# Sparse attention then top-1 MoE on one core: three groups of two score tiles a pair instead of four groups

## The chip, the cores and the metric

The kernel runs on one core of a Trainium2 chip. The metric is device time in microseconds from the first to the last instruction of a launch. Before the change it is 352.2 us, the median of three runs (350.9 to 353.01). The profile is one execution of its own, with a span of 355.5 us and a mean granted TensorE clock of 0.988.

A core has five engines, each with its own in-order queue: PE (matmul; its weight loads are shown as PEld), DVE (vector), ACT (scalar and activation), POOL (GpSimd) and SP (here it issues DMAs). They wait for each other through semaphores.

## The reference

The inputs are q, k and v of 4 batches x 8 heads x 768 positions x 64, and a mixture of 8 experts. Attention looks only at a few chunks of 32 keys. For each query an upper bound of its score with each chunk is made from the chunk's element-wise minimum and maximum, and the six causal chunks of the highest bound are kept:

```python
ub = np.sum(np.maximum(q[:, :, :, None, :] * k_min[:, :, None, :, :], q[:, :, :, None, :] * k_max[:, :, None, :, :]), axis=-1)
...
top_chunks = np.argsort(ub, axis=-1)[..., -top_k:]
...
mask = sel & (pos[:, None] >= pos[None, :])
...
attn = attn / (np.sum(attn, axis=-1, keepdims=True) + 1e-09)
return np.matmul(attn, v).astype(np.float32)
```

The heads are then put side by side into rows of 512. Each of the 3072 rows goes to the one expert with the highest gate logit, a relu MLP 512 to 1024 to 512, and is scaled by that expert's softmax probability.

## The kernel before

**Tiling.** Two heads of one batch make a pair, so there are NP = 16 pairs; i is the pair, hp = i % 4 its place in the batch, n = i + 1 and m = i + 2. A pair's 768 queries are two halves of 384 (qb 0 and 1). The scores are made transposed, keys on the partitions, in seven units u (line 286): units 0 and 1 belong to query half 0, units 2 to 6 to half 1. For each unit:

- `scores(i, u)` (L298, PE) multiplies KTE by QSB into a PSUM tile `ps`, of which there are two. Rows 64 and up of KTE and QSB carry the chunk mask, so a chunk that was not chosen is pushed down inside the same matmul.
- `exps(i, u)` (L314, ACT) takes the exponential into SBUF. Units 0 and 2 go to a tile `Pa` (four buffers), which also becomes the accumulator of the half's denominators; the others go to `Pr`, also four buffers. On blocks of the diagonal POOL then clears what is not causal (L318).
- `av(i, u)` (L331, PE) multiplies by V into `po`, of which there is one PSUM bank, used by half 0 and then by half 1.
- `add(i, u)` (L339, DVE) adds the unit into the accumulator. A `Pr` buffer is free when its `av` and its `add` are done.
- `o_ev(i, qb)` (L346 on DVE, L344 on ACT) copies `po` to an `ot` tile.

**Preparation of later pairs** is mixed in. `k_mm`, `k_v`, `k_a` and `q_mm`, `q_v`, `q_a` transpose k and q of pair m on PE, take chunk maxima and minima on DVE (L197, L198), and copy on DVE, ACT and POOL. Where DVE and ACT both read one PSUM bank, the one that stands second in the code waits for the first. `kse` builds the matrix for the bounds. `ub` (L238, PE) makes the bounds, `ub_a` (L245, ACT) copies them to `ubT`, `sel_mm` (L250, PE) transposes them, `sel_v` (L256, L264, L267, DVE) takes the sixth largest and compares. `mask` (L274, PE) transposes the choice, and `mask_a` (L280, ACT) writes it into the mask rows of QSB, which must be done before that pair's scores 0.

**Routing of earlier pairs** is mixed in too. `ud` (PE) and `ud_a` (L380, ACT) gather the denominators and logits of pair i - 1, `lgp_mm` (L385, PE) transposes them, `lgp_v` (L391, L395, DVE) takes reciprocals and scales the logits, and their sums go to POOL later (`sums_`, L403 and L406). `x_mm` and `x_v` (L415, PE; L420, DVE) write the normalised output rows, half 0 one pair late and half 1 two pairs late. In the pairs with hp = 1 and b > 0, the router pairs 5, 9 and 13, the rows of the batch before get their experts: `logits`, `rank_mm`, `expo` (ACT), `rank_v`, `gates`. Rows are scattered to DRAM by POOL. All transposes and bounds share three PSUM buffers of tag `m`, in the order in which they are asked for.

**Order.** All five engines run under a manual schedule (L807): each executes its instructions in the order in which the Python code records them, so the order of calls in the loop over i is the order of every queue. Before the change, that loop has an inner loop over four groups g: scores 2 and 3; scores 4 and 5, then 6; the mask and AV 4 and 5; and scores 0 and 1 of the next pair with the rest of its preparation and AV 6. The output of one pair is finished while the next one is started.

**After attention**, from about 232 us, gathered rows of each expert go through `up` and `down` (L641, L653). The diff does not touch this part, nor `first_pair`.

Of the kernel before, what the change touches and what calls it, by code (L numbers as in the profile page):

```python
# [24 lines left out]
def kernel(  # L25
# [24 lines left out]
    NP = B * H // 2  # L50
# [108 lines left out]
    late, sums_ = [], []  # L159
# [518 lines left out]
    def pieces(i, n):  # L678
        for _ in range(min(n, npiece[i])):
            load_w(next(wnext))  # L680
            npiece[i] -= 1
# [121 lines left out]
    def run(d, j, name, *a):  # L803
        if j in d:
            d[j][name](*a)

    with tc.manual_schedule(engines={PE, POOL, SP, DVE, ACT}):  # L807
        first_pair()
        early_table = table(True)
        for i in range(NP):  # L810
            b, hp = divmod(i, HP)
            n, m = i + 1, i + 2
            router = hp == 1 and b > 0
            if router:
                logits, expo, gates, rank_mm, rank_v, _ = route[b - 1]
            if i == NP - 1:
                for j in range(2):
                    gather(j)
                    x_in(j)
            for g in range(4):  # L820
                if (i, g) == (0, 0):
                    pass
                elif g == 0:
                    if i < NP - 1 and not (hp == 2 and b > 0):
                        pieces(i, 2 if router else 1)
                    if router:
                        logits()
                    for u in (2, 3):
                        scores(i, u)
                        exps(i, u)  # L830
                    run(rout, i - 2, "x_mm", 1)

                    xv_first = i < NP - 1 and (hp != 2 or b == 0)
                    if xv_first:
                        run(rout, i - 2, "x_v", 1)
                    if i < NP - 1:
                        add(i - 1, 5)
                    add(i - 1, 6)
                    if not xv_first:
                        run(rout, i - 2, "x_v", 1)  # L840
                    av(i, 0)
                    av(i, 1)
                    dve_ot = not router and i < NP - 2
                    if dve_ot or i == NP - 1:
                        o_ev(i, 0, not dve_ot)
                    add(i, 1)
                    run(prep, n, "ub")
                    run(prep, n, "ub_a")
                    if not dve_ot and i < NP - 1:
                        o_ev(i, 0, True)  # L850
                    if i < NP - 1:
                        load(n, "v")
                elif g == 1:
                    for u in (4, 5):
                        scores(i, u)
                        exps(i, u)
                    run(prep, n, "sel_mm")
                    if i > 0:
                        run(prep, m, "k_mm", 0)
                        run(prep, m, "k_a", 0)  # L860
                    if router:
                        rank_mm()
                    run(prep, n, "sel_v")
                    if router:
                        expo()
                        rank_v()
                        gates()
                    if i > 0:
                        run(prep, m, "k_v", 0)
                    av(i, 2)  # L870
                    av(i, 3)
                    add(i, 3)
                    flush(late)
                    if i < NP - 1:
                        pieces(i, 4)
                    scores(i, 6, True)
                    exps(i, 6)
                    if i == NP - 1:
                        for j in (2, 3):
                            gather(j)  # L880
                            x_in(j)
                        pieces(i, 4)
                    run(rout, i - 1, "ud")
                    run(rout, i - 1, "ud_a")
                    if i == NP - 2:
                        next(early_table)
                elif g == 2:
                    if i == 0:
                        run(prep, m, "k_mm", 0)
                    run(prep, n, "mask")  # L890
                    run(prep, n, "mask_a")
                    if i == 0:
                        run(prep, m, "k_v", 0)
                        run(prep, m, "k_a", 0)
                    av(i, 4)
                    av(i, 5)
                    if not router:
                        add(i, 4)
                    if i == NP - 2:
                        for _ in early_table:  # L900
                            pass
                    flush(sums_)
                    if i == NP - 1:
                        meta(0)
                        meta(1)
                        gather(4)
                        gather(5)
                else:
                    run(rout, i - 1, "lgp_mm")
                    run(rout, i - 1, "x_mm", 0)  # L910
                    if n < NP:
                        for u in (0, 1):
                            scores(n, u)
                            exps(n, u)
                    if i == NP - 2:
                        add(i, 5)
                    run(rout, i - 1, "lgp_v")
                    run(rout, i - 1, "x_v", 0)
                    run(prep, m, "k_mm", 1)
                    run(prep, m, "k_v", 1)  # L920
                    run(prep, m, "k_a", 1)
                    for hf in range(2):
                        run(prep, m, "q_mm", hf)
                        run(prep, m, "q_v", hf)
                        run(prep, m, "q_a", hf)
                    if i + 3 < NP:
                        load(i + 3, "k", "q")
                    av(i, 6)
                    o_ev(i, 1, i >= NP - 2)
                    run(prep, m, "kse")  # L930
                    if router:
                        add(i, 4)
                    if hp == 0 and b > 0:
                        flush(sums_)
                if 1 <= hp <= 2 and b > 0 and spread[4 * (hp - 1) + g]:
                    route[b - 1][5](spread[4 * (hp - 1) + g])
        rt = rout[NP - 1]
        r = route[B - 1]

        def nxt(j):  # L940
            meta(j - XB)
            gather(j)

        rout[NP - 2]["x_mm"](1)
        rout[NP - 2]["x_v"](1)
        nxt(6)
        nxt(7)
        flush()
        up(0)
        up(1)  # L950
        rt["ud"]()
        rt["ud_a"]()
        x_in(4)
        up(2)
        x_in(5)
        rt["lgp_mm"]()
        rt["lgp_v"]()
        for hf in range(2):
            rt["x_mm"](hf)
            rt["x_v"](hf)  # L960
        flush()
        nxt(8)
        r[0]()
        r[1]()
        r[2]()
        down(0)
        up(3)
        x_in(6)
        nxt(9)
        r[3]()  # L970
        r[4]()
        meta(6)
        meta(7)
        for _ in table(False):
            pass
        gathers = {3: (10,), 4: (11,), 5: (12, 13)}
        for j in range(1, NS):
            if j == NS - 4:
                up(NS - 1)
            down(j)  # L980
            if j < 3:
                r[5](range(3 * j - 3, 3 * j))
            for k_ in gathers.get(j, (j + 8,) if 5 < j < NS - 8 else ()):
                if k_ > 11:
                    meta(k_ - XB)
                gather(k_)
            if j + 8 >= NS and j + 4 < NS:
                meta(j + 4)
            if j + 3 < NS - 1:
                up(j + 3)  # L990
            if j + 6 < NS:
                x_in(j + 6)

        _, more = nc.values_load_multi_w_load_instructions(  # L994
            late_i[0:1, 0:1], min_val=0, max_val=NB,
            skip_runtime_bounds_check_because="a count of tiles that the table itself adds up")
        with tc.If(more[0] > NS - NA) as _:
            for j in range(NS, JT):
                gather(j)
                x_in(j)  # L1000
                meta(j)
            for j in range(NS, JT):
                up(j)
            for j in range(NS, JT):
                down(j)
# [37 lines left out]
```

The softmax here doesn't subtract the row's maximum and nothing guards it: scores larger than these inputs give would overflow.

## Time and profile before

| | before |
|---|---|
| median of three runs | 352.2 us (350.9 to 353.01) |
| span of the profiled execution | 355.5 us |
| attention loop | to about 232 us |
| from one L391 to the next, ordinary pair | 13.2 to 13.5 us |
| the same, router pairs and those after them | 14.3 to 14.8 us |
| exponential of a unit (L314, ACT) | 0.81 us |
| DVE add of a whole unit (L339) | 0.98 us |
| mask copy (L280, ACT) | 0.69 us, two a pair |

A row of the timeline gives the start, the time covered, engine and line, the operation with what it writes and reads, the number of merged instructions, and in brackets the idle time before it with what ended it. The time of several merged rows is that of their union. [...] A busy PE is not PE at its peak, since the ends of its pipelined matmuls are modelled.

### The profile page before, as it was taken

What the parts mean: (1) busy time and instruction counts of PE and PEld (TensorE: products, weight loads), DVE (VectorE), ACT (ScalarE), POOL (GpSimd) and SP (SyncE); (2) the same over time, 40 slices, a digit from 0 to 9 for tenths busy, and PEclk for the clock granted to TensorE, in tenths of its full rate; (3) what the DMA queues carried; (4) which work ended last, traced back from release to release, by engine and by line L of the source; (5) the groups of instructions that cost most, each with busy time, mean ns of one, the idle gap of its engine ahead of it and who ended that gap; (6) DMA issues with size and microseconds to landing.
All of it is one profiled execution on the core that took longest, in us unless ns stands there. A gap on an engine that the chain in (4) does not pass through costs nothing. (4 is left out here: it accounts for less than half of the span.)

```text
span 355.5 us, 7585 instructions
## 1 busy us (share of the span) xinstructions
PE 329.2 (93%) x2382; PEld 177.2 (50%) x2392; DVE 229.5 (65%) x776; ACT 230.4 (65%) x373; POOL 186.7 (53%) x300
## 2 busy tenths in 40 slices
PE   7889999999999999999999999977995899999992
PEld 7545656556555555555565555534441344444440
DVE  6688999999999999999999999941730000000000
ACT  2588788788796887886887977613323454544551
POOL 8515434536475437284355477583574556655323
PEclk9999999999999999999999999989998999999999
DMA  9998998899585897765979954969694999998962
GB/s 175 205 209 152 167 184 169 153 190 167 104 211 113 161 178 155 152 171 114 186 137 181 182 122 113 209 124 197 137 227 121 227 185 216 194 231 160 216 154 80
DMA packets 132071, 59.83 MB, mean 168 GB/s; under 512 B 122811, under 2 KB 122813, under 8 KB 132032
## 3 DMA queue, kind: packets, MB, share of 16 engines
q1 hardware_dynamic: 120640, 29.91, 43.5%
q0 software_dynamic: 11392, 29.42, 40.0%
q8 instruction: 21, 0.34, 0.4%
q14 instruction: 18, 0.15, 0.1%
HBM read 56.14 MB, written 10.51 MB: 188 GB/s over the span
## 5 line engine op out<-in xcount | busy, mean ns | idle before, releaser
L339 DVE TENSOR_TENSOR Pa<-Pa,Pr 128x768 f32<-128x768 f32 (+2 forms) x109 | 80.5, 742 | 4.3
L318 POOL TENSOR_SCALAR_AFFINE_SELECT Pr<-Pr 128x256 f32<-128x256 f32 x78 | 36.9, 492 | 77.9 <-ACT Pr L314 77.9
L314 ACT ACTIVATE Pr<-ps 128x768 f32<-128x768 f32 x79 | 62.6, 819 | 10.7 <-ACT KTE L203 4.3
L653 PE MATMUL py<-w_all,hT 128*128 x220 | 52.4, 379 | 3.0 <-issue 1.7
L298 PE MATMUL ps<-QSB,KTE 128*128 128x384 bf16 (+4 forms) x352 | 50.4, 283 | 1.5 <-ACT Pr L314 0.2
L661 POOL DMA_INDIRECT out_dram<-y,ti_all x28 | 28.0, 1001 | 37.2 <-ACT y L660 32.1
L298 PEld LDWEIGHTS <-KTE 128*128 128x128 bf16 (+1 forms) x352 | 26.5, 102 | 28.4 <-issue 22.0
L641 PE MATMUL ph<-w_all,KTE 128*128 x116 | 31.1, 413 | 6.3 <-ACT h__3986 L644 3.6
L653 PEld LDWEIGHTS <-hT 128*128 128x128 bf16 x224 | 21.8, 98 | 29.5 <-issue 1.8
L314 ACT ACTIVATE Pa<-ps 128x768 f32<-128x768 f32 x32 | 26.0, 812 | 14.0 <-PE ps L298 12.6
L660 ACT ACTIVATE y<-py,gt_all 128x512 f32<-128x512 f32 x27 | 18.6, 687 | 25.0 <-PE py L653 19.4
L203 ACT ACTIVATE KTE<-pk 64x384 bf16<-64x384 f32 x60 | 29.3, 488 | 7.1 <-DVE kmn L198 6.7
L493 POOL DMA_INDIRECT xs_dram<-xrow,sli x24 | 25.6, 1065 | 7.8 <-issue 5.7
L641 PE MATMUL ph<-w_all,QSB 128*128 x94 | 22.6, 379 | 1.6 <-DMA QSB<-xgqT 1.5
L641 PEld LDWEIGHTS <-KTE 128*128 128x128 bf16 x120 | 12.3, 104 | 23.0 <-issue 9.6
L280 ACT ACTIVATE QSB<-pm 24x640 bf16<-24x640 bf16 x30 | 20.8, 692 | 2.8 <-PE pm L274 2.1
L614 DVE TENSOR_TENSOR ti_all<-xgqA,inv_i 128x1 int32<-128x1 int32 x9 | 1.4, 160 | 30.7 <-DMA xgqA<-xs_dram,grow 26.1
L157 POOL DMA_DIRECT2D w_all<-in_moe_w_dram x32 | 21.1, 663 | 0.0
L197 DVE TENSOR_REDUCE kmx<-pk 128x12 f32<-128x384 f32 x32 | 17.6, 549 | 3.2 <-PE pk L192 3.0
L593 POOL DMA_INDIRECT xgqT<-xs_dram,grow x14 | 14.8, 1058 | 9.1 <-issue 6.2
L593 POOL DMA_INDIRECT xgqA<-xs_dram,grow x14 | 14.4, 1029 | 8.6 <-issue 4.7
L614 DVE TENSOR_TENSOR ti_all<-xgqT,inv_i 128x1 int32<-128x1 int32 x8 | 1.3, 159 | 25.7 <-DMA xgqT<-xs_dram,grow 20.9
(318 smaller groups left out, 635.9 us busy)
## 6 DMA issues: line engine op xcount, KB each, us to landing
w_all<-in_moe_w_dram POOLq DMA_DIRECT2D x32, 512.0 KB
out_dram<-y,ti_all POOLq DMA_INDIRECT x28
t__115<-in_k_dram SPq DMA_DIRECT2D x2, 192.0 KB
t__118<-in_q_dram SPq DMA_DIRECT2D x2, 192.0 KB
t__121<-in_v_dram SPq DMA_DIRECT2D x2, 192.0 KB
t__218<-in_k_dram SPq DMA_DIRECT2D x2, 192.0 KB
t__240<-in_q_dram SPq DMA_DIRECT2D x2, 192.0 KB
t__243<-in_v_dram SPq DMA_DIRECT2D x2, 192.0 KB
```

The source lines that it names most:

```text
L157: nc.gpsimd.dma_start(out=dst, in_=src.rearrange("(c p) f -> p c f" if n < 2 else "(p c) f -> p c f", p=128))
L203: nc.scalar.activation(kte[0:64, hd, ts(hf, 384)], pt[64 * hd:64 * hd + 64, :], AF.Copy, bias=0.0, scale=0.125)
L280: nc.scalar.activation(qsb[64:64 + NCH, hd, 128:S], s["pm"][32 * hd:32 * hd + NCH, 128:S], AF.Copy)
L298: nc.tensor.matmul(ps[ds(h * n, n), hd, ds(c0, w)], lhsT=kte[:, hd, ds(kb * 128 + h * n, n)], rhs=qsb[:, hd, ds(qb * 384 + 384 - w, w)], s ...
L314: nc.scalar.activation(P[:], ps[:, :, 0:384], AF.Exp)
L318: nc.gpsimd.affine_select(out=pd, in_=pd, pattern=[[0, 2], [1, 128]], compare_op=ALU.is_ge, fill=0.0, base=0, channel_multiplier=-1)
L339: nc.vector.tensor_tensor(acc[:, :, 384 - w:384], acc[:, :, 384 - w:384], P[:, :, ds(c0, w)], ALU.add)
L493: d = nc.gpsimd.indirect_dma_start(out=xs_dram[:], out_offset=bass.IndirectOffsetOnAxis(ap=sli[:, u:u + 1], axis=0), in_=bst[b][f"xrow{u % ...
L593: d = nc.gpsimd.indirect_dma_start(out=xg_bufs[j % XB].bitcast(I32), out_offset=None, in_=xs_dram[:], in_offset=bass.IndirectOffsetOnAxis( ...
L641: nc.tensor.matmul(ph[:, fh, :], lhsT=xT[:, c, :], rhs=w_all[:, ds(wo + (c * F + fh * 512), 512)], start=(c == 0), stop=(c == NDC - 1), sk ...
L653: nc.tensor.matmul(py[:], lhsT=hT[:, c, :], rhs=w_all[:, ds(wo + (W1W + c * DM), DM)], start=(c == 0), stop=(c == NFC - 1))
L661: d = nc.gpsimd.indirect_dma_start(out=out[:], out_offset=bass.IndirectOffsetOnAxis(ap=fs[j]["ti"], axis=0), in_=y[:], in_offset=None, bou ...
```

## The change

The four groups of a pair are replaced by three that are written out, with two score tiles and then the AV products of earlier units each. It has four purposes: to put the next scores in front of an AV product, so that PE has work while exponentials and selects of that product are under way; to give the bounds a longer lead, by making those of pair m at the end of pair i where before those of pair n were made in the first group; to put the selection ahead of the adds of unit 6 and 1; and to put the mask's transposes and copies next to scores 4 and 5. The diff, cut to its core (`rows_out` holds the scatters, whose place among the groups stays):

```diff
-for g in range(4):
...
-    elif g == 0:
...
-        for u in (2, 3):
-            scores(i, u)
-            exps(i, u)
-        run(rout, i - 2, "x_mm", 1)
...
-            run(rout, i - 2, "x_v", 1)
-        if i < NP - 1:
-            add(i - 1, 5)
-        add(i - 1, 6)
...
-        av(i, 0)
-        av(i, 1)
...
-            o_ev(i, 0, not dve_ot)
-        add(i, 1)
-        run(prep, n, "ub")
-        run(prep, n, "ub_a")
...
-    elif g == 1:
-        for u in (4, 5):
-            scores(i, u)
-            exps(i, u)
-        run(prep, n, "sel_mm")
-        if i > 0:
-            run(prep, m, "k_mm", 0)
-            run(prep, m, "k_a", 0)
-        if router:
-            rank_mm()
-        run(prep, n, "sel_v")
-        if router:
-            expo()
-            rank_v()
-            gates()
-        if i > 0:
-            run(prep, m, "k_v", 0)
-        av(i, 2)
-        av(i, 3)
-        add(i, 3)
-        flush(late)
...
-        scores(i, 6, True)
-        exps(i, 6)
...
-        run(rout, i - 1, "ud")
-        run(rout, i - 1, "ud_a")
...
-    elif g == 2:
...
-        run(prep, n, "mask")
-        run(prep, n, "mask_a")
...
-        av(i, 4)
-        av(i, 5)
-        if not router:
-            add(i, 4)
...
-        flush(sums_)
...
-    else:
-        run(rout, i - 1, "lgp_mm")
-        run(rout, i - 1, "x_mm", 0)
-        if n < NP:
-            for u in (0, 1):
-                scores(n, u)
-                exps(n, u)
...
-        run(rout, i - 1, "lgp_v")
-        run(rout, i - 1, "x_v", 0)
-        run(prep, m, "k_mm", 1)
-        run(prep, m, "k_v", 1)
-        run(prep, m, "k_a", 1)
-        for hf in range(2):
-            run(prep, m, "q_mm", hf)
-            run(prep, m, "q_v", hf)
-            run(prep, m, "q_a", hf)
...
-        av(i, 6)
-        o_ev(i, 1, i >= NP - 2)
-        run(prep, m, "kse")
-        if router:
-            add(i, 4)
-        if hp == 0 and b > 0:
-            flush(sums_)
+if i > 0:
...
+    for u in (2, 3):
+        scores(i, u)
+        exps(i, u)
+    run(rout, i - 2, "x_mm", 1)
+    run(prep, n, "sel_mm")
+    if i < NP - 1:
+        add(i - 1, 5)
+
+    xv_first = i < NP - 1 and (hp != 2 or b == 0)
+    if xv_first:
+        run(rout, i - 2, "x_v", 1)
+    run(prep, n, "sel_v")
+    if not xv_first:
+        run(rout, i - 2, "x_v", 1)
+    av(i, 0)
+    av(i, 1)
+    o_ev(i, 0, not dve_ot)
+    add(i - 1, 6)
+    add(i, 1)
...
+for u in (4, 5):
+    scores(i, u)
+    exps(i, u)
+if i == 0:
+    run(prep, n, "sel_mm")
+    run(prep, n, "sel_v")
+else:
+    run(prep, m, "k_mm", 0)
+    run(prep, m, "k_a", 0)
+    run(prep, n, "mask")
+    run(prep, n, "mask_a")
+    if router:
+        rank_mm()
+        expo()
+        rank_v()
+        gates()
+    run(prep, m, "k_v", 0)
+av(i, 2)
+av(i, 3)
+add(i, 3)
+flush(late)
...
+scores(i, 6, True)
+exps(i, 6)
...
+run(rout, i - 1, "ud")
+run(rout, i - 1, "ud_a")
...
+run(rout, i - 1, "lgp_mm")
+run(rout, i - 1, "x_mm", 0)
+if not router:
+    add(i, 4)
...
+flush(sums_)
...
+run(rout, i - 1, "lgp_v")
+run(rout, i - 1, "x_v", 0)
+run(prep, m, "k_mm", 1)
+if n < NP:
+    scores(n, 0)
+    exps(n, 0)
+    scores(n, 1)
+run(prep, m, "k_v", 1)
+run(prep, m, "k_a", 1)
+for hf in range(2):
+    run(prep, m, "q_mm", hf)
+    run(prep, m, "q_v", hf)
+    run(prep, m, "q_a", hf, 0)
+if n < NP:
+    exps(n, 1)
+for hf in range(2):
+    run(prep, m, "q_a", hf, 1)
...
+run(prep, m, "kse")
+av(i, 4)
+av(i, 5)
+av(i, 6)
+o_ev(i, 1, i >= NP - 2)
+run(prep, m, "ub")
+run(prep, m, "ub_a")
+if router:
+    add(i, 4)
+if hp == 0 and b > 0:
+    flush(sums_)
```

The order of calls that follows from it, for an ordinary pair: scores 2 and 3; x of pair i - 2; transposes and selection for n; AV 0 and 1 and their copy; adds of unit 6 of pair i - 1 and of unit 1; scores 4 and 5; the first k half of m; the mask of n; AV 2 and 3; scores 6; `ud` and `lgp` of pair i - 1; the second k half; scores 0 and 1 of n; q of m with the exponential of unit 1 between its copies; AV 4, 5 and 6; bounds of m.

## Prediction

> **What bounds the kernel now.** I read the page for the engines' shares, then the stages, then the timeline of one ordinary pair (pair 3), each step beside the code.
>
> ```profile
> PE 329.2 (93%) x2382; PEld 177.2 (50%) x2392; DVE 229.5 (65%) x776; ACT 230.4 (65%) x373; POOL 186.7 (53%) x300
> ```
>
> Over the span only PE looks full. By stage it is different (columns: stage, its length, busy PE, PEld, DVE, ACT, POOL, then clock, DMA share, GB/s):
>
> ```profile
> 60.00:80.00 20.00, 19.86 (x174) 10.97 (x170) 18.80 (x60) 17.07 (x30) 8.40 (x16) 1.00 0.89 174
> 300.00:320.00 20.00, 19.89 (x93) 9.07 (x93) 1.37 (x13) 9.55 (x13) 11.85 (x12) 1.00 0.96 206
> ```
>
> In the attention stage, which is all that the diff edits, DVE is busy 18.8 of 20 us. From 33 to 232 us it idles 11.4 us, of which 8.4 us are 570 gaps of 15 ns on average between neighbours, and only 2.9 us are gaps with an outside releaser. PE's 19.9 says less: its records overlap (four matmuls of 0.54 and 0.49 us fit in 0.87 us). So DVE sets the pace of a pair, 13.5 us, and PE and ACT run ahead of it. Timeline of one pair:
>
> ```profile
> 62.80 1.53 ACT L314 ACTIVATE Pr<-ps 128x768 f32<-128x768 f32 x2
> 63.92 0.45 DVE L256 TENSOR_TENSOR ubm<-pt,cbias 128x288 f32<-128x288 f32 x1
> ...
> 65.72 0.81 ACT L314 ACTIVATE Pr<-ps 128x768 f32<-128x768 f32 x1 [0.54 <-ACT KTE L203]
> ...
> 66.61 1.48 POOL L318 TENSOR_SCALAR_AFFINE_SELECT Pr<-Pr 128x256 f32<-128x256 f32 x2 [0.38 <-ACT Pr L314]
> ...
> 66.87 0.49 ACT L380 ACTIVATE ud<-pu 128x384 f32<-128x384 f32 x1 [0.34 <-PE pu L374]
> ...
> 67.39 1.41 ACT L280 ACTIVATE QSB<-pm 24x640 bf16<-24x640 bf16 x2
> ...
> 68.06 1.55 POOL L406 TENSOR_TENSOR lg<-lg,lgt 128x96 f32<-128x96 f32 x2
> ...
> 69.64 0.42 DVE L395 TENSOR_TENSOR lgt<-pl,rec 128x96 f32<-128x96 f32 x2 [0.41 <-POOL lg L406]
> ...
> 69.98 0.55 DVE L420 TENSOR_TENSOR xrow<-px,rec 128x384 bf16<-128x384 f32 x1
> ...
> 71.55 0.98 ACT L203 ACTIVATE KTE<-pk 64x384 bf16<-64x384 f32 x2 [0.39 <-DVE kmn L198]
> ```
>
> The reader is to see that DVE's rows stand without idle time except 0.41 us before lgt, while ACT's idle bits cost nothing; and that everything is in lockstep through short waits, so the order in each queue is the schedule.
>
> **What the Trainium skill says.** "Perfetto Trace Analysis", Identifying the Most-Contended Engine: occupancy is a fair measure for Vector and Scalar, matmul busy time is not one for Tensor; the overlap above agrees. "PSUM — Partial Sum Buffer", Engine vs sequencer instructions: the Scalar, Vector and GpSimd queues are strict FIFO; all rows here stand in program order. "SBUF — State Buffer", Who interferes with whom: a DVE instruction with two SBUF inputs contends with a GpSimd instruction that reads SBUF; agreed, the two selects at 66.61 took 0.40 us and, beside an add, 1.12 us. "TensorE: Matmul & The Clock Gate", What's actually happening: after an idle window of about 3.4 us the array falls to half clock; the page grants 0.99 here, so no run shows it yet.
>
> **The change, part by part.** No instruction is added or removed; all of it is order. Moves that only shift PE work (AV of units 4 and 5 behind the next scores; the mask transposes ahead of AV 2) cost PE nothing by themselves, and PE is not the bound. What matters are four moves on DVE and ACT, which form one closed loop. I follow it from S, the start of the first-half x multiply L420 (69.98 above), with durations start to start out of this pair.
>
> 1. DVE after S: 0.47, two reduces of the second k half, the last ends at S+1.48. ACT's KTE copies wait for it: S+1.57 (71.55). As before.
> 2. ACT then had two KTE copies and four q copies, the exponential of unit 1 already done (70.36). Now: KTE 2 x 0.50, qA 2 x 0.51, exponential of unit 1 0.69, QSB 2 x 0.50, and then the new ubT of pair i+2 at S+5.29, done at S+5.74. PE arrives earlier: AV 4 to 6 from S+1.06 (3 x 0.65), bounds 1.08, scores 2 and 3 0.75, x transposes 0.4, that is S+5.3.
> 3. The sel transposes, which DVE needs for the selection, now stand in the next pair's first group and wait for this ubT (before, ubT had most of a pair's head start). 5.80 + 0.55, so DVE's selection starts at S+6.39. Before it DVE has only kse, ot, add 5 and x: it is idle about 1.6 us between S+2.8 and S+6.39.
> 4. Selection 2.03, ot 0.47, then add 6 of the last pair in two parts, ends S+10.1. Before, add 6 stood ahead of all these.
> 5. Pr has four buffers, so the exponential of unit 5 writes the one that unit 6 of the last pair held: it needs add 6. It starts at S+10.13, where it would otherwise go at S+7.7 to 9.1. Queued behind it on ACT: KTE 2 x 0.50, the mask copies L280 2 x 0.72 (before, these came behind ud), the exponential of unit 6 0.69, ud 0.49: done at S+14.45. DVE waits too: its first k reduce must follow ACT's KTE copies of the same bank, S+11.88 instead of 11.1.
> 6. PE's lgp transposes wait for ud: 14.51 + 0.58, the reciprocal at S+15.1 + 0.27, lgt 0.34, the next L420. From here S' = S+15.7.
> 7. lgt also waits for POOL: two selects of unit 6 and two sums. Unit 6's exponential ends at S+14.08. Without contention 0.36+0.36+0.39+0.47 gives lgt at 15.7; as in the pair above (end 66.54, lgt 69.64) it is 17.2. The first select meets add 4 (to S+14.8) and the rest nothing, so I take lgt 16.3, S' = S+16.6. Both ends stay for the range: 15.7 and 17.5.
>
> A pair of this kind goes from 13.5 to 16.6 us: +3.1 (2.2 to 4.0). L420's first-half spacing before is 13.5 for pairs 2, 3, 4, 7, 8, 11, 12: 7 x 3.1 = 21.7.
>
> Router pairs 5, 9, 13 (14.4 before): the head's logits need POOL's last sums, which are flushed at the pair's end behind the selects of unit 1; that exponential now ends at S+4.4, so the sums end at S+6.1. Then on DVE logits 1.33 (86.75 to 88.08), add 5 0.98, x 0.47, selection 2.03, add 6 1.2: S+12.1. On ACT exponential 0.69, KTE 1.0, masks 1.43, the small exponential ends S+15.5; on DVE gates 0.70 (94.76 to 95.46), which now wait for it, k reduces 0.93, add 3 0.87, rec and lgt 0.60: S' = S+18.7. +4.3, at least +1.8 if logits are not late. 3 x 4.3 = 12.9.
>
> Pairs 6 and 10: as ordinary ones, with x_v behind the selection (0.47): 17.1 against 14.4, 2 x 2.7 = 5.3. Pair 1 has no sums to wait for: 15.7 against 13.5, +2.3 (0 to 3). Pair 14 has no k and q preparation but the table, which hides much: +1 (0 to 2). After 232 us nothing is edited; it moves later as a whole, its weights landing no later, at zero cost.
>
> Sum: 21.7 + 12.9 + 5.3 + 2.3 + 1 = 43 us, 352.2 + 43 = 395. The lower ends give 7 x 2.2 + 3 x 1.8 + 2 x 1.8 = 24, so 376; the upper ones 28 + 12.9 + 7 + 3 + 2 = 53, so 405.
>
> **The rivals.**
> - A, the gaps close: PE gets longer runs and nobody waits. DVE has 2.9 us of outside waits to lose, so 349 at best. For it: the lgt waits of 0.41 are real, and PE and ACT have slack. Against: DVE's list is as long as before and already almost without gaps, and the four moves put waits into it. 6%, a third of it inside 0.5%.
> - B, the head alone costs: DVE loses 1.6 us before the selection, but the late exponential of unit 5 is absorbed, since ACT was busy only 11.2 of 13.5 us in this pair. 12 x 1.5 = 18, so 370. Against: ACT's slack lies in front of the wait; behind it five copies and two exponentials follow in a FIFO queue up to ud, and DVE has only k, add 3 and add 4 meanwhile. 14%.
> - C, the clock falls too: PE waits from about S+12.1 (ud products done) to S+14.5, 2.4 us, and in router pairs to S+16.9, 4.8 us. If the array then runs at half clock for a window in half of the pairs, each loses about 1.5 us on its next group: 395 + 6 x 1.5 = 404. 10%.
>
> **How the numbers follow.** The loop as worked out has 70%, A 6%, B 14%, C 10%. The predicted time is the loop's, 395. A range from 377 to 405 leaves out A and most of B, about 18%, and takes in the bounds of lgt and of the router pairs. Faster 0.04, same 0.02, slower 0.94.
>
> **What would show it.** Right: L420's first-half spacing of 15.7 to 17.5 us in ordinary pairs and above 16 in router pairs; DVE busy about 15.5 of 20 us; selection L256 waiting for PE's pt; exponential Pr waiting for DVE's add about 1 us once a pair; k reduces waiting for ACT KTE, lgt for POOL. Wrong: DVE still above 18 of 20 us, or pairs longer with L256 first without a wait. The prediction falls if unit 5's exponential does not stop for add 6, for then ud comes 2 us earlier and the pair is B's; or if POOL's selects and sums take less or more than between 1.6 and 3.1 us.

## The result and the profile after

The changed kernel takes 402.19 us (median of four runs, 400.12 to 403.6) against 352.61 us (350.9 to 353.85) for the kernel before on the same chip. The ratio is 1.1405, with a 95% interval of 1.1332 to 1.1479: slower by 49.6 us. Forecast were 395 us and a range of 377 to 405. Medians here and below are of all runs of a kernel and ratios of its fast runs alone: one of the four runs of experiment 4, at 400.51 us, and a few others count as slow.

The granted clock on the page of the kernel before, then engine shares and granted clock of the changed one:

```profile
PEclk9999999999999999999999999989998999999999
...
PE 337.3 (85%) x2382; PEld 191.3 (48%) x2392; DVE 232.3 (58%) x776; ACT 230.3 (58%) x373; POOL 182.1 (46%) x300
...
PEclk9999898898989898899998989998999999999999
```

Every engine has its old count of instructions and, within 3%, its old busy time on DVE, ACT and POOL, in a span that is 42.6 us longer. Nobody does more work; everybody waits more. New are the eights that run through the attention stage in the clock. The same two stages as before the change:

```profile
60.00:80.00 20.00, 17.46 (x127) 11.60 (x128) 14.85 (x44) 11.38 (x20) 6.67 (x15) 0.84 0.71 136
340.00:360.00 20.00, 19.89 (x92) 9.08 (x93) 1.23 (x12) 9.90 (x12) 12.07 (x12) 1.00 1.03 212
```

In attention DVE falls from 18.8 to 14.85 of 20 us, and the expert stage is as busy as before (PE 19.89 of 20 us in both). Where the time went is read from the spacing of one reciprocal L391 to the next, in us (n is the number of pairs in the row):

| | before | after | added, all n | forecast |
|---|---|---|---|---|
| first L391 (pair 1) | at 42.2 | at 43.9 | 1.7 | 2.3 |
| ordinary pairs, n = 7 | 13.2 to 13.5 | 15.8 to 17.0 | 24.0 | 21.7 |
| router pairs, n = 3 | 14.8 | 19.7 to 20.1 | 15.5 | 12.9 |
| pairs 6 and 10 | 14.3, 14.5 | 16.6, 15.9 | 3.8 | 5.3 |
| pair 14 | 18.4 | 19.6 | 1.3 | 1 |
| last two | 6.2, 12.9 | 8.2, 14.7 | 3.8 | 0 |
| sum | | | 50.0 | 43 |

The loop alone accounts for the 49.6 us. (The spans differ by less than the medians because the profiled execution of the kernel before took 106.8 us from its first L653 to the end, that of the changed kernel 100.8; so the part after attention varies from execution to execution.)

The timeline of the changed kernel, pair 3 again, from one L420 to the next:

```profile
78.83 0.55 DVE L420 TENSOR_TENSOR xrow<-px,rec 128x384 bf16<-128x384 f32 x1
...
79.65 0.81 ACT L314 ACTIVATE Pa<-ps 128x768 f32<-128x768 f32 x1 [2.91 <-PE ps L298]
...
83.06 0.56 DVE L346 COPY ot<-po 128x384 f32<-128x384 f32 x1 [0.93 <-PE po L331]
...
84.20 0.44 ACT L245 ACTIVATE ubT<-pu 128x320 f32<-128x320 f32 x1 [0.38 <-PE pu L238]
...
85.21 0.56 DVE L420 TENSOR_TENSOR xrow<-px,rec 128x384 bf16<-128x384 f32 x1 [0.64 <-PE px L415]
...
85.69 0.45 DVE L256 TENSOR_TENSOR ubm<-pt,cbias 128x288 f32<-128x288 f32 x1
...
88.16 2.27 DVE L339 TENSOR_TENSOR Pa<-Pa,Pr 128x512 f32<-128x512 f32 x4
...
89.42 0.81 ACT L314 ACTIVATE Pr<-ps 128x768 f32<-128x768 f32 x1 [1.14 <-DVE Pa L339]
...
90.12 0.97 ACT L203 ACTIVATE KTE<-pk 64x384 bf16<-64x384 f32 x2
...
91.12 1.40 ACT L280 ACTIVATE QSB<-pm 24x640 bf16<-24x640 bf16 x2
91.13 0.56 DVE L197 TENSOR_REDUCE kmx<-pk 128x12 f32<-128x384 f32 x1 [0.70 <-ACT KTE L203]
...
93.25 0.48 ACT L380 ACTIVATE ud<-pu 128x384 f32<-128x384 f32 x1
93.43 1.20 POOL L318 TENSOR_SCALAR_AFFINE_SELECT Pr<-Pr 128x256 f32<-128x256 f32 x2 [1.14 <-ACT Pr L314]
...
93.79 0.90 PE L385 MATMUL pl<-ident_f,ud 128*128 128x128 f32 x3 [2.54 <-ACT ud L380]
...
94.60 0.85 POOL L406 TENSOR_TENSOR lg<-lg,lgt 128x96 f32<-128x96 f32 x2
94.73 0.23 DVE L391 RECIPROCAL rec<-pl 128x12 f32<-128x12 f32 x1 [0.72 <-PE pl L385]
...
95.48 0.42 DVE L395 TENSOR_TENSOR lgt<-pl,rec 128x96 f32<-128x96 f32 x2 [0.53 <-POOL lg L406]
...
95.82 0.55 DVE L420 TENSOR_TENSOR xrow<-px,rec 128x384 bf16<-128x384 f32 x1
```

Neighbouring rows of one engine can overlap by some 0.1 us (ACT at 89.42 takes 0.81 us, the next row starts at 90.12), so sums are taken from starts. Read it as a relay. The late bounds (84.20) let the selection start at 85.69. Behind the selection stand ot and add 6 (the row at 88.16 holds adds 6 and 1, two instructions each; those of add 6 end at 89.30); when add 6 ends, the exponential of unit 5 starts at once (89.42, after 1.14 us without work). Behind that ACT has KTE, mask copies, the exponential of unit 6 and ud, all without a gap to 93.73; PE has stood still for 2.54 us until ud came. Then L391, lgt, L420 and the next turn. Each step's wait in brackets is the step before it. The same in the sums of all waits (us in total, times, longest), the first line from the kernel before, the others from the changed one:

```profile
ACT Pr L314 <- DVE Pa L339: 1.8, 2, 1.4
...
PE pl L385 <- ACT ud L380: 33.8, 15, 2.6
...
ACT Pr L314 <- DVE Pa L339: 19.8, 14, 2.3
...
DVE ot L346 <- PE po L331: 13.5, 14, 1.5
...
DVE rk L480 <- ACT ex L449: 7.3, 3, 2.5
DVE kmx L197 <- ACT KTE L203: 6.9, 10, 0.7
...
DVE lgt L395 <- POOL lg L406: 6.7, 7, 2.1
```

The clock's eights, taken apart in windows around this pair (columns as in the prediction; the clock is the third number from the end):

```profile
76.70:80.10 3.40, 3.31 (x16) 2.79 (x17) 2.15 (x7) 0.49 (x2) 1.68 (x4) 0.51 0.66 132
80.10:93.80 13.70, 11.16 (x100) 6.37 (x98) 10.83 (x32) 10.59 (x19) 4.04 (x9) 1.00 0.67 128
93.80:97.20 3.40, 3.40 (x16) 2.88 (x17) 2.15 (x7) 0.56 (x1) 1.57 (x4) 0.50 0.79 149
```

For 3.4 us around the end of the wait for ud, PE runs at half speed: here lgp, the x and k transposes, and the first scores. There are eleven such windows in the loop, the last of them in pair 14; each starts between 0.3 us before and 2.1 us after the end of a wait for ud, and four waits have none. The kernel before has no half-clock window in its loop and two behind it, at 237.7 and 271.8 us.

### The profile page after: what moved, and what is told of

Same layout as the page of the kernel before. It is cut to its first block, busy times and chain, and to the rows that moved or that the text cites. A ratio compares the mean times of both kernels' runs of the same rounds, so it can differ in the third digit from the quotient of the medians.

```text
span 398.1 us, 7550 instructions
## 1 busy us (share of the span) xinstructions
PE 337.3 (85%) x2382; PEld 191.3 (48%) x2392; DVE 232.3 (58%) x776; ACT 230.3 (58%) x373; POOL 182.1 (46%) x300
## 5 line engine op out<-in xcount | busy, mean ns | idle before, releaser
L318 POOL TENSOR_SCALAR_AFFINE_SELECT Pr<-Pr 128x256 f32<-128x256 f32 x78 | 38.7, 515 | 129.0 <-ACT Pr L314 129.0
L314 ACT ACTIVATE Pr<-ps 128x768 f32<-128x768 f32 x79 | 63.9, 812 | 33.4 <-DVE Pa L339 19.8
L339 DVE TENSOR_TENSOR Pa<-Pa,Pr 128x768 f32<-128x768 f32 (+2 forms) x109 | 78.8, 736 | 2.9
L298 PE MATMUL ps<-QSB,KTE 128*128 128x384 bf16 (+4 forms) x352 | 55.2, 309 | 0.8 <-ACT QSB L280 0.7
L653 PE MATMUL py<-w_all,hT 128*128 x220 | 52.2, 379 | 2.2 <-DMA hT<-h__4696 1.0
L298 PEld LDWEIGHTS <-KTE 128*128 128x128 bf16 (+1 forms) x352 | 30.1, 111 | 28.3 <-issue 20.1
L385 PE MATMUL pl<-ident_f,ud 128*128 128x128 f32 x48 | 10.4, 335 | 33.9 <-ACT ud L380 33.8
L653 PEld LDWEIGHTS <-hT 128*128 128x128 bf16 x224 | 21.8, 98 | 28.6 <-DMA hT<-h__4696 1.4
L641 PE MATMUL ph<-w_all,KTE 128*128 x116 | 28.0, 379 | 5.5 <-DVE gt_all L616 2.8
L385 PEld LDWEIGHTS pl<-ident_f,ud 128*128 128x128 f32 x48 | 5.9, 161 | 39.6 <-ACT ud L380 39.4
L346 DVE COPY ot<-po 128x384 f32<-128x384 f32 x25 | 13.9, 554 | 13.5 <-PE po L331 13.5
L593 POOL DMA_INDIRECT xgqT<-xs_dram,grow x14 | 14.6, 1040 | 14.6 <-issue 4.2
```

What stands on the lines that cost most here:

```text
L298: nc.tensor.matmul(ps[ds(h * n, n), hd, ds(c0, w)], lhsT=kte[:, hd, ds(kb * 128 + h * n, n)], rhs=qsb[:, hd, ds(qb * 384 + 384 - w, w)], s ...
L314: nc.scalar.activation(P[:], ps[:, :, 0:384], AF.Exp)
L318: nc.gpsimd.affine_select(out=pd, in_=pd, pattern=[[0, 2], [1, 128]], compare_op=ALU.is_ge, fill=0.0, base=0, channel_multiplier=-1)
L339: nc.vector.tensor_tensor(acc[:, :, 384 - w:384], acc[:, :, 384 - w:384], P[:, :, ds(c0, w)], ALU.add)
L641: nc.tensor.matmul(ph[:, fh, :], lhsT=xT[:, c, :], rhs=w_all[:, ds(wo + (c * F + fh * 512), 512)], start=(c == 0), stop=(c == NDC - 1), sk ...
L653: nc.tensor.matmul(py[:], lhsT=hT[:, c, :], rhs=w_all[:, ds(wo + (W1W + c * DM), DM)], start=(c == 0), stop=(c == NFC - 1))
```

## Experiments

Ratios are against the kernel before, measured alongside, whose median was 352.2 to 353.5 us (357.3 in experiment 6). "Undone" means in the changed kernel; what came "back" is the difference to its 402.19 us, which was measured at another time, so that a difference of 2 or 3 us hardly stands out. "Loop" is the prediction's chain, "clock" the half clock alone.

**1. Add 6 ahead of the selection, undone alone.**

```diff
     if i < NP - 1:
         add(i - 1, 5)
+        add(i - 1, 6)
...
-    add(i - 1, 6)
     add(i, 1)
```

> The changed kernel with one move undone: the add of unit 6 stands ahead of the selection again. LOOP (the pair is set by the closed chain selection, add 6, exponential of unit 5, ACT copies, ud, lgp): that exponential stops waiting for DVE (1.1 us a pair gone, 2.2 in router pairs), ud comes that much earlier, PE's wait for it shrinks from 2.5 to about 1.4 us, and with it the half-clock windows go; 17.0 us a pair becomes 14.7 to 15.5, in all 375 to 383 us. CLOCK (the half clock makes the loss, the add is beside the point): 398 to 404 unless the gap closes. HEAD (only the late bounds and selection cost): no change, 399 to 404, or slower, since the selection is pushed back by 1.2 us.

Measured: 388.52 us, ratio 1.1024 (1.0951 to 1.1098), so 13.7 us came back. Ordinary pairs take 14.3 to 15.1 us, as the loop theory had it; router pairs stay at 20.1 to 21.3. Its wait of the exponential for the add:

```profile
ACT Pr L314 <- DVE Pa L339: 3.1, 6, 0.8
```

19.8 us of waiting are down to 3.1, and no half-clock window is left in the ordinary pairs (those at 101.8, 166.6 and 231.5 lie in router pairs). So the gain holds two things, the wait for the add and the half clock; experiment 3 tells them apart. The link is real; the total was missed on the high side (375 to 383 expected), as the three router pairs became 1.9 us longer together.

**2. Mask copies behind ud, undone alone.**

```diff
     run(prep, n, "mask")
-    run(prep, n, "mask_a")
...
 run(rout, i - 1, "ud_a")
+if i > 0:
+    run(prep, n, "mask_a")
```

> The changed kernel with the two mask copies on ACT moved back behind ud. LOOP: 1.4 us less stand between the exponential of unit 5 and ud, but DVE's k reduces and adds 3 and 4 still run to about the present start of the reciprocal, so 0.7 to 1.7 us a pair: 380 to 393 us. CLOCK: PE's wait for ud shrinks to 1.1 us, the half clock goes, 1.2 us in ten pairs: 390. HEAD: no change, 399 to 404.

Measured: 395.88 us, 1.1227 (1.1154 to 1.1301): 6.3 us back, less than expected. Ordinary pairs fall to 15.3 in four of seven cases and stay at 16.5 to 17.0 in the others, and the wait for the add grows to 22.8 us, as if the next pair reached the same closed door sooner. Here too no half-clock window is left in the ordinary pairs. Together they are 6.5 us shorter, no more than the half clock alone is worth there (6.2, experiment 3); a price of the copies by themselves is not shown in them. The router pairs are 4.6 us shorter together, but 6.1 us are lost again at the first L391, in pairs 6 and 10 and from pair 14 on.

**3. PE kept busy while it waits for ud.** Thirty small matmuls go into unused columns of po's bank (the tile is widened to 512 columns for it). The output is then not the reference's (the matmuls share the bank in which the AV products are still being summed), and rows can go to other experts, so the spacings in the loop say more here than the total.

```diff
 run(rout, i - 1, "ud_a")
...
+if 0 < i < NP - 1:
+    for _ in range(30):
+        nc.tensor.matmul(st[i]["po1"][:, 384:512], lhsT=ones_b[:], rhs=ones_b[:], start=True, stop=True, skip_group_check=True)
```

> The changed kernel with 30 extra small bf16 matmuls (about 1.7 us, their result is never read; they go to columns of the output bank that are not used) between ud and lgp on PE, where PE now waits 2.5 us. LOOP: the chain stays and only the share of the half clock goes: spacing 15.8 us instead of 17.0 in about ten pairs, so 387 to 392 us, granted clock 0.99. CLOCK: most of the 50 us come back, under 375. If PE were the bound, the extra work would cost 13 times 1.7 us: 420.

Measured: 394.59 us, 1.1181 (1.1105 to 1.1257). The stage that had 0.84 now reads:

```profile
60.00:80.00 20.00, 18.89 (x171) 12.30 (x171) 15.78 (x47) 12.81 (x22) 7.43 (x16) 1.00 0.78 157
```

Full clock, 7.6 us back; ordinary pairs take 15.4 to 16.2, router pairs 20.0 to 20.1 (19.7 to 20.1 unfilled). The half clock is a consequence of the wait, worth 0.8 to 1.5 us in six of the ordinary pairs, 6.2 in all, and not the main cause: the clock theory (below 375) falls. The total is 3 us above the loop's 387 to 392. Of the 14.0 us that experiment 1 takes from the ordinary pairs, 6.2 are thus half clock and 7.8 the wait for the add itself.

**4. AV of units 4 and 5 back between ud and lgp, alone.** The same gap, filled with the work that the kernel before had there.

```diff
 run(rout, i - 1, "ud_a")
...
+av(i, 4)
+av(i, 5)
...
-av(i, 4)
-av(i, 5)
 av(i, 6)
```

> The changed kernel with AV of units 4 and 5 alone put back between ud and lgp. LOOP: PE's wait for ud is filled with 1.3 us of real work, so the half clock goes in ordinary pairs (1.2 us each), and the bounds and the next scores come 1.3 us earlier, of which ACT's own queue up to ubT lets 0.1 to 0.5 us through; add 6 still stops the exponential of unit 5: 15.3 to 15.8 us an ordinary pair, 380 to 392 us. If AV 4 and 5 were the main part of the loss: under 370. If they are harmless where they stand: 398 to 404.

Measured: 394.86 us, 1.1222 (1.1141 to 1.1303). The spacings are those of experiment 3 (15.44, 15.78, 16.23 against 15.44, 15.77, 16.23; router pairs 20.0 in both). Moving AV 4 and 5 cost its share of half clock, some 7 us, and nothing else as long as add 6 holds the chain. The total is again 3 us above the range of the loop. As this kernel leaves nothing out, it also supports the total of experiment 3.

**5. The kernel before, with add 6 made late.** For this the selection moves in front of scores 5, and with it its transposes on PE.

```diff
-                    add(i - 1, 6)
...
-                    for u in (4, 5):
-                        scores(i, u)
-                        exps(i, u)
+                    scores(i, 4)
+                    exps(i, 4)
                     run(prep, n, "sel_mm")
+                    run(prep, n, "sel_v")
+                    if i > 0:
+                        add(i - 1, 6)
+                    scores(i, 5)
+                    exps(i, 5)
...
-                    run(prep, n, "sel_v")
```

> The kernel before, with one move of the change alone: the selection between scores 4 and 5, and the add of unit 6 behind it. LOOP: the exponential of unit 5 waits for the add, about 3 us later than before, and ACT's queue behind it carries the delay to ud; 2 to 3 us a pair, 378 to 392 us. HEAD and CLOCK: ACT's slack of 2 us a pair takes it up, 351 to 360 us.

Measured: 372.78 us, 1.0561 (1.0492 to 1.0629), 19.3 us slower. Its waits:

```profile
ACT Pr L314 <- DVE Pa L339: 27.2, 15, 2.7
...
DVE ubm L256 <- PE pt L250: 7.9, 10, 1.1
```

1.8 us an exponential, and ordinary pairs at 15.24 instead of 13.2 to 13.5, with no half clock in the loop. An add behind the selection is enough to make the loop. The price is for both moves: the second line, the selection waiting for its transposes, was 1.3 us in the kernel before. Per pair it is a little under the 2 to 3 us that were expected, and the total is below the 378 to 392.

**6. The kernel before, with the bounds alone made early.**

```diff
-                    run(prep, n, "ub")
-                    run(prep, n, "ub_a")
...
                     o_ev(i, 1, i >= NP - 2)
                     run(prep, m, "kse")
+                    run(prep, m, "ub")
+                    run(prep, m, "ub_a")
```

> The kernel before, with the early bounds alone: the bounds of pair i + 2 and their copy at the pair's end, and nothing else moved. LOOP: the bounds, 1.1 us of PE, now stand ahead of scores 2 and 3 and of the x transposes that DVE's next multiply needs; DVE, whose list fills the pair, idles 0.5 to 1.0 us there and nothing gives it back: 13.9 to 14.4 us an ordinary pair, 358 to 366 us. HARMLESS (PE runs ahead and DVE does not notice; what was left of the loss with the orders and AV put back comes from elsewhere): 351 to 355 us.

Measured: 382.68 us against 357.28, 1.0726 (1.0622 to 1.0829): 25.4 us slower, in the expected direction, but two to four times as far. The kernel before was slower and less even here than elsewhere (353.5 to 360.4); in the profiles the last L391 comes 27.2 us later, which agrees. Timeline of one pair's end:

```profile
63.42 0.26 DVE L210 TENSOR_TENSOR KSD<-kt,bm 128x96 f32<-128x96 f32 x1
...
63.83 0.76 PE L238 MATMUL pu<-qT,KSD 128*64 128x320 f32 x4 [1.55 <-DVE KSD L210]
...
66.35 0.56 DVE L420 TENSOR_TENSOR xrow<-px,rec 128x384 bf16<-128x384 f32 x1 [2.67 <-PE px L415]
```

At the pair's end PE reaches the bounds before DVE has made their matrix KSD, and waits 1.55 us; scores 2 and 3 and the x transposes are queued behind it, and DVE waits 2.67 us for these. Over the loop DVE waits 22.7 us there. In the changed kernel AV 4 and 5 stand in front of the bounds and fill that wait: no wait of PE for KSD is left, and DVE waits 4.5 us for the x transposes. So little of this cost carries over; the expectation had left it out.

**7. The small exponential of the router early, undone alone.**

```diff
         exps(i, u)
+    if router:
+        expo()
...
-        expo()
         rank_v()
```

> The changed kernel with the small exponential of the router pairs recorded right after the exponential of unit 3 instead of behind the mask copies. QUEUE (in router pairs DVE's rank waits 2.4 us for this exponential, which stands at the end of ACT's queue behind unit 5): the wait goes, DVE runs rank and gates while ACT copies, and each of the three router pairs is 1.5 to 2.4 us shorter: 395 to 398 us. DVE-FULL (the router pairs are long because DVE has 2 us more to do): no change, 400 to 404.

Measured: 399.55 us, 1.1263 (1.1175 to 1.1352). Router pairs fall from 19.7 to 20.1 to 17.8 to 18.1 us, 2.0 each, and the rank's wait for the exponential is gone. Of these 6 us, 3.6 reach the last L391 of the profile and 2.6 the median, which the runs' scatter (394.7 to 400.9) does not tell from nothing: pair 11's turn, at full clock before (15.77), now meets a half-clock window (17.01), and pair 14 and the last spacing are longer by 0.8 and 1.2 us.

**8. Add 6, mask copies, exponential and the last sums, all four orders undone.** Edits of 1, 2 and 7, and the flush of the last sums moved from the pair's end to right behind the first-half L420.

> The changed kernel with four orders put back on ACT, DVE and POOL and nothing else: the add of unit 6 ahead of the selection, mask copies behind ud, the small exponential early, the last sums of a batch ahead of the selects of unit 1. PE's order and the early bounds stay as changed. LOOP: ordinary pairs 14.0 to 14.7 us instead of 17.0, router pairs 16 to 17.5 instead of 20, in all 362 to 374 us. If the early bounds and the later AV products are harmless, 352 to 357. If the parts only shift the wait to the next one in the loop, 380 to 389.

Measured: 378.93 us, 1.0751 (1.0701 to 1.08), 23.3 us back. Ordinary pairs 14.6 to 14.8, router pairs 18.3 (one 16.7). Waits:

```profile
ACT Pr L314 <- PE ps L298: 24.6, 15, 4.2
...
DVE ot L346 <- PE po L331: 10.9, 14, 1.0
...
ACT Pr L314 <- DVE Pa L339: 2.7, 1, 2.7
```

The wait for the add is gone but for one, and others stand in its place: exponentials for scores, ot for AV. The loop now seems to run through PE's order. That was the "next wait" case of the expectation, whose range it misses by 1 us. In the ordinary pairs the four orders together bring no more than add 6 alone (103.3 us over seven of them, 103.7 in experiment 1); what the others bring lies in the router pairs.

**9. As 8, and AV 4 and 5 back as in 4.**

> The kernel with the four orders put back, and AV of units 4 and 5 put back too, between ud and lgp where PE waits for ud. With the four orders back, ordinary pairs took 14.8 us, and unit 4's exponential waited 1.4 us for scores 4, which stand on PE behind AV 4 to 6, the bounds and the selection's transposes. LOOP (the closed chain now runs through PE, and AV 4 and 5 are 1.3 us of it): 13.5 to 13.9 us an ordinary pair, 358 to 368 us in all. BOUNDS (the early bounds hold it, not the AV products): 374 to 380 us.

Measured: 371.12 us, 1.0512 (1.044 to 1.0584): 7.8 us more back, between the two ranges of the expectation. Ordinary pairs 14.3 to 14.8, router pairs 16.4. Some 19 us remain. What is still changed there is above all the early bounds, the selection in front of scores 4, the mask's transposes in front of AV 2, the exponential of unit 1 between the q copies, and the order on PE around scores 0 and 1. I did not separate them. One wait points to the early bounds, which now reach PE before the copies of q that they read are done; the kernel before has no such wait:

```profile
PE pu L238 <- ACT qA L228: 12.5, 13, 1.1
```

**10 to 12. Is DVE's list really the pace of the kernel before?** The prediction said so; then relief of DVE should show. First, the copy ot of half 0 always on ACT; then the sums of POOL ahead of the selects of unit 6, which takes away the lgt waits; then both.

```diff
-                    dve_ot = not router and i < NP - 2
+                    dve_ot = False
```

```diff
                     flush(late)
+                    flush(sums_)
```

> The kernel before, with the copy of the first query half out of PSUM on ACT in all pairs, as router pairs have it. It tests what bounds the kernel before. DVE-BOUND: 0.47 us less on DVE in about ten pairs, 346 to 349.5 us. PE-BOUND or bound by the chain through ACT: 352 to 356 us, no gain or a loss.

> The kernel before, with POOL's two logit sums ahead of the selects of unit 6 instead of behind them. DVE-BOUND: the six waits of 0.41 us before lgt go, 349.5 to 351 us. Otherwise 352 to 354, or a little more if the sums now hold the port while DVE takes the selection's compare.

> The kernel before, with the first half's copy on ACT and POOL's sums early, together. Each alone gained nothing: with the copy on ACT the wait of lgt for POOL's sums grew from 0.41 to 0.77 us. HAND-OVER (DVE's relief was taken up by that wait): together 0.4 to 0.5 us an ordinary pair come out, 344 to 349 us. CHAIN (a loop through ACT of the same length as DVE's list holds the pair): 351 to 355 us.

Measured: 354.34 us, 1.0021 (0.9996 to 1.0046); 354.62 us, 1.0055 (1.0031 to 1.0078); both 352.35 us, 1.0005 (0.9981 to 1.0029). No gain in any total. Groups by form on DVE, from 42 to 152 us, of the kernel before (instructions, busy us, mean ns, idle before):

```profile
L339 DVE TENSOR_TENSOR Pa<-Pa,Pr 128x768 f32<-128x768 f32 x23 | 22.4, 975 | 0.3
...
L346 DVE COPY ot<-po 128x384 f32<-128x384 f32 x14 | 7.7, 548 | 0.0
L267 DVE TENSOR_TENSOR nsel<-ubm,top 128x288 bf16<-128x288 f32 x8 | 3.7, 462 | 0.3
L395 DVE TENSOR_TENSOR lgt<-pl,rec 128x96 f32<-128x96 f32 x16 | 3.4, 253 | 1.9 <-POOL lg L406 1.6
```

and of the kernel with both edits:

```profile
L339 DVE TENSOR_TENSOR Pa<-Pa,Pr 128x768 f32<-128x768 f32 x24 | 24.8, 1035 | 0.3
L267 DVE TENSOR_TENSOR nsel<-ubm,top 128x288 bf16<-128x288 f32 x8 | 5.2, 653 | 0.3
L346 DVE COPY ot<-po 128x384 f32<-128x384 f32 x8 | 4.4, 548 | 0.0
L395 DVE TENSOR_TENSOR lgt<-pl,rec 128x96 f32<-128x96 f32 x16 | 3.4, 253 | 0.7
```

Over eight pairs DVE is spared 3.3 us of copies and 1.2 us of waits. It gives back 1.5 us in the compare L267 and 24 x 60 ns = 1.4 us in whole-unit adds, and 1.6 us or 0.2 us a pair would be left. The compare now runs beside POOL's cast of q, and both got longer (the two casts 0.94 to 1.17 us): that agrees with the Trainium skill, "SBUF — State Buffer", Who interferes with whom, where a DVE instruction with two SBUF inputs contends with a GpSimd instruction that reads SBUF. The lost time is counted as busy. DVE still sets the pace with both edits: over the twelve spacings from pair 2 to pair 13 its waits for others fall from 2.6 to 0.3 us, and the spacings from 166.7 to 164.9. These 1.8 us are lost again at the first L391 (0.7 us later) and from pair 14 on (2.0 us). So the list on DVE is full, but its length depends on what POOL does at the same moment.

No version that was run beats the kernel before.

## Why the prediction was right, and where not

**The loop (steps 1 to 6): the mechanism right, step by step; the size helped by luck.** Times from S = 78.83: selection L256 predicted at 6.39, measured 6.86; exponential of unit 5 at 10.13, measured 10.59; ud done 14.45, measured 14.90; L391 15.1, measured 15.9; lgt 16.3, measured 16.65; S' 16.6, measured 16.99. The 0.45 us from the selection to ud come from ahead of it: the bounds are queued behind AV 4 to 6, and these start at S+2.03 where I had S+1.06, because PE is at half clock until about S+1.3; in experiment 3, at full clock, the same selection starts at S+6.08. L391 is late by another 0.35 us for lgp at half clock, and POOL's shorter term takes that back. DVE is busy 14.85 of 20 us where 15.5 was expected. Rivals A and B fall: there are waits where A had none, and the exponential of unit 5 stops for add 6, which B had absorbed. The mark named as decisive, that unit 5's exponential stops about 1 us for add 6, was 1.14 us. Experiments 1 and 5 show the link by cutting and by making it. At full clock, however, ordinary pairs take 15.4 to 16.2, so the loop itself costs 17.7 us in the seven of them where the prediction had 21.7; the 24.0 measured were reached only with the half clock, which the loop did not contain.

**POOL's term (step 7): right.** I had lgt wait 0.9 us for the sums, from 15.4 (L391 and its 0.27) to 16.3. In pair 3 it was 0.53, as L391 was late there; before four other turns of the same profile it is 0.88 to 0.89.

**Rival C, given 10%, came true on top of the loop.** Its 404 us is nearer to the measured 402.2 than the loop's 395. It had half clock in half of the pairs, which is what came: six ordinary pairs, from waits of 2.5 us. It costs nothing measurable in router pairs (20.04 and 20.06 us in pairs 9 and 13, both with it and in experiment 3). I had put it at 1.5 us times 6; experiments 3 and 4 give 7.3 to 7.6 us. The Trainium skill, "TensorE: Matmul & The Clock Gate", What's actually happening, gives a free-running window of 3413 ns and half clock after an idle one. The length agrees (3.41 us), and so does the free running, as the last section shows; but in the loop no window was idle all through, so here a mostly idle one was enough. Without this loss the changed kernel takes 394.6 to 394.9, where the loop was put at 395; that agreement is partly luck, since ordinary pairs were put too long (16.6 against 15.4 to 16.2) and router pairs too short.

**Router pairs: +5.2 us each, not +4.3.** The step had only the gates wait for the small exponential. Timeline of the changed kernel, pair 5:

```profile
107.54 0.81 ACT L314 ACTIVATE Pr<-ps 128x768 f32<-128x768 f32 x1 [2.23 <-DVE Pa L339]
...
110.64 0.24 ACT L449 ACTIVATE ex<-sh 128x48 f32<-128x48 f32 x1
...
110.92 0.21 DVE L480 TENSOR_TENSOR rk<-pr,base_e 128x48 f32<-128x48 f32 x1 [2.43 <-ACT ex L449]
```

Already the rank's first instruction L480 waits for it, so rank work that I counted as done comes behind. The code has the reason: rk is written into the one buffer of tag `sh`, which the exponential reads. Experiment 7 gives 2.0 us a router pair back by moving that exponential.

**The last two pairs: 0 predicted, +3.8 measured.** This term was missed outright: the prediction has no step for it. The last spacing alone lies between 11.8 and 17.3 us in the kernels run here, and it was not traced to the edits, so part of it may be variation; that stays open.

**What bounds the kernel before: too simple.** "DVE sets the pace" was enough to see that waits put into DVE's list cost time. It does not follow that relief of DVE gains any, and in experiments 10 to 12 no gain shows in the total. Two readings on the way were off. The 8.4 us of small gaps on DVE lie in 160 gaps of some 50 ns; the other instructions among the 570 have none. And a half clock was to be seen in the profile before, at 237.7 and 271.8 us, behind the loop.

**How the 50 us divide.** By the medians, add 6 undone alone gives 13.7 us, the AV products 7.3, the mask copies 6.3, the router's exponential 2.6; all of these and the last sums together 31. The first three of these cannot be added up, since each of them ends the half clock in the ordinary pairs and so contains its 6.2 us. The seven ordinary pairs tell more. Together they take, in us:

| kernel | seven ordinary pairs |
|---|---|
| before | 93.7 |
| changed | 117.7 |
| half clock gone (experiments 3 and 4) | 111.4 |
| mask copies undone (2) | 111.2 |
| add 6 undone (1) | 103.7 |
| all four orders undone (8) | 103.3 |
| AV 4 and 5 as well (9) | 102.0 |

Of the 24.0 us, 6.2 go with the half clock, 7.8 more with add 6, 1.7 with the other orders and AV 4 and 5, and 8.3 remain. Made in the kernel before, the late add costs 19.3 us in all and the early bounds 25.4; these cannot be added to the rest, because a wait that another one covers costs nothing twice. The share of the early bounds within what remains was not measured in the changed kernel.

## What to carry to other kernels

Where all engines run in a fixed order, follow each buffer's release around one full turn of the loop: an instruction that frees a rotating buffer (here an add) must not stand behind one that waits for something made late in the same turn. Cut or make one such link alone, in both kernels, before believing a list of causes; what a link costs depends on the waits around it. And do not read a gapless engine as time that can be taken away: look at whether its instructions are longer than they are when their neighbours are silent.

## What the runs showed of the hardware that was not expected

- A PE wait of 1.9 to 2.6 us, once a pair, was followed by 3.41 us at half clock, eleven times in the loop. The starts of these windows (42.61, 59.68, 76.74, 93.81, 114.29 us and so on) lie whole multiples of 3.413 us apart: 5, 5, 5, 6, 5, 5, 5, 15, 5 and 10. So they lie on a grid that runs on by itself, and the wait does not start them. Counted on this grid, PE's records cover 0.26 to 0.45 of the window ahead of each of the eleven, and at least 0.46 of every other one at full clock after the first 20 us. In the other kernels run here the line lies somewhere between 0.42 and 0.56.
- So it matters where on the grid a wait falls. The wait ahead of pair 11's turn, 2.59 us up to 200.4, was as long as the others but lay across a boundary at 199.62, which left 0.46 and 0.78 of the two windows covered. No half clock followed, and that turn took 15.77 us, as at full clock in experiment 3.
- While the half clock came every turn, windows lay 17.07 us apart, five times 3.41, and six ordinary pairs took 16.9 to 17.0, where in experiments 3 and 4, at full clock, the same pairs take 15.4, 15.8 or 16.2. In experiment 7 all seven take 16.85 to 17.01. It looks as if the period of the pairs had locked to the clock's windows; no run tested that by itself.
- The DVE compare L267 took 0.46 us with no cast of POOL or only the tail of one beside it, and 0.75 us beside both casts, which themselves went from 0.94 to 1.17 us for two.
